# Attention scores as two 64-row matmuls side by side, and one sum instruction for two steps

## The chip, the cores and the metric

The kernel runs on one core of a Trainium2 chip. Its time is the device time of one execution in microseconds (us); shown is the median of several executions. TensorE (PE) multiplies matrices, and its weight loads are listed apart (PEld); VectorE (DVE), ScalarE (ACT) and GpSimd (POOL) do the elementwise work; SyncE (SP) and ScalarE's queue issue DMAs.

## What is computed

Four batches of eight heads of attention over 576 positions with head size 64, with a threshold in the scores, and then two feed-forward layers over all 2304 tokens (512 wide, 2048 inside):

```
scores = (1/sqrt(64)) * q @ k.T                      # per head, 576 x 576
thresh = max(scores, row) - tau
scores = where(scores >= thresh, scores, -1e9)
attn   = exp(scores - max(scores, row)); attn /= sum(attn, row) + 1e-9
x = concat over heads of (attn @ v)                  # 2304 x 512
h = x @ w_in;  x = (relu(h) * relu(h)) @ w_out       # layer 1
h = x @ w2_in; out = max(0.01*h, h) @ w2_out         # layer 2
```

## The kernel before, in words

The two heads of a pair are worked on together. A pair has nine **steps**: four blocks of 128 query rows for each head, and one step that holds the last 64 rows of both heads (the remainder). There are 16 pairs, so 144 steps. `step(i)` issues what leads to the masked row: the scores of 128 query rows against all 576 keys go to a PSUM tile `s` of two banks, 288 keys in each (L585); VectorE takes the row maximum `nb` (L595), ScalarE the exponential `e` (L596), `th` is the threshold (L597, VectorE or GpSimd), VectorE masks and sums (L602), a small instruction `t` adds 1e-9 to the sum and scales it (L605, VectorE or GpSimd), and after every second step a reciprocal `r` of both sums follows (L608). There are two tiles `s`, so a step's scores wait for the mask of the step before last. `rest` then scales the rows, turns them, and `values` multiplies them with v.

The pairs come in three kinds. The first four (batch 0) scale in place, turn the rows with TensorE transposes against an identity matrix into `pt` (L627, L628), copy them to `PT` and multiply with v in single precision, in 64-column matmuls (L688). The first six pairs (list `nat`, steps 0 to 53) have single-precision scores; pairs four and five then use half-precision rows that DMAs turn. The last ten pairs split q and k into a high and a low part; their score matmuls (tiles KH and KL) are not changed.

For the first six pairs `prep` loads K of both heads into one tile KH, head 0 in partitions 0 to 63 and head 1 in partitions 64 to 127, 576 keys wide, and scales it. The tile Q2 holds for each head its 64 rows in the same partitions, with zeros in the other 64 (memsets, L484). A matmul over all 128 partitions thus gives one head's scores; a step issues two, one for each half of the keys. In the remainder step there are four, each with 64 columns of weights.

The order of the work is not written by hand. Every instruction is recorded with a priority (step number plus an offset from the table CFG), a cost, and the engines that may run it; `Plan.order` then simulates the engines and places one instruction after the other, and where several engines may run it the prices in CFG weigh them. Beside the attention run the splitting of layer 1's weights into high and low parts (`w_block`, tiles `wraw`), and from batch 1 on part of layer 1 (`ffn`, L736 and L762). After the attention come the rest of layer 1 (L1166, L1208) and layer 2 (L1055, L1133).

Of the kernel before, what the change touches and what calls it, by code (L numbers as in the profile page):

```python
# [13 lines left out]
ALU = mybir.AluOpType  # L14
# [4 lines left out]
P = 128  # L19
UP = 32768.0  # L20
# [7 lines left out]
           {'V': 2.058, 'A': 0.5, 'G': 0.597},  # L28
           {'V': 1.454, 'A': 0.877, 'G': 1.005},
           {'V': 4.321, 'A': 0.378, 'G': 0.428},  # L30
           {'V': 1.956, 'A': 0.969, 'G': 2.867},
           {'V': 3.46, 'A': 0.884, 'G': 4.561},
           {'V': 3.025, 'A': 1.381, 'G': 2.849}],
    lead1=0.344, xsg0=[0, 1], lbm=8, lb=[[0, 3, 5, 6], [1, 5], [0, 4], [2, 7]], xsm=4, xsg=[1, 2], dq=0.417, xu=False, pqk=-3.957,
    pd1=1.458, pex=1.266, pd2=1.468, ph=3.893, pl=-2.254, hu=True, bg=6.244, lead=4.309, w0=25.544, wstep=1.408, fend=1.015, tol=-0.227,
    hor=-0.102, xlead=5.334, nb=3, eb=4, pb=3, ptb=3, kvb=3, nat=[0, 1, 2, 3, 4, 5], nav=4, two=False, vb=2, tmb=1, gb=2, xb=1,
    w2step=-3.901, nf=[12, 12, 12, 12], wo=2.009, wold=[9, 10, 16], yal=40.578, xl2=26.294, xp=5, sp=2.609, ws=-16.879, ww=20.813, zc=3.74,
    th=0.397, x2l=2.921, sg0=1.043, sgstep=1.158, zb=1.416, zin=1.434, zout=1.386, slack=0.02, slackd=0.985, wrb=3, r1b=1, xrb=1,
# [226 lines left out]
def mmr(n):  # L265
    return (n + 32) / 2400.0
# [11 lines left out]
def tile_kernel(ctx: ExitStack, tc: tile.TileContext, qT, kT, vv, w1, w2, tau, eye, out):  # L278
    nc = tc.nc
    B, H, D, S = qT.shape  # L280
# [4 lines left out]
    S2 = S // 2  # L285
    MAIN = S // P
    REM = S - MAIN * P
    NH = (S + P - 1) // P
    QB = S + REM
# [47 lines left out]
    def dma(o, i, r, w, prio, nbytes, q=nc.sync, **k):  # L337
        return op(("S", 0.06, lambda: q.dma_start(out=o(), in_=i())), r, w, prio, dma=move(nbytes), **k)
# [126 lines left out]
    def prep(n):  # L465
# [6 lines left out]
        o.Q, o.pad = Q, []  # L472
# [3 lines left out]
        if n in CFG["nat"]:  # L476
# [3 lines left out]
            for h in range(2):  # L480

                c0, c1 = (0, S) if len(what) > 5 else (0, 2 * P) if what is head and h == 0 else (REM, REM + 2 * P) if what is head else (2 * P, S) if h == 0 else (0, S)
                z = lambda h=h, c0=c0, c1=c1: qs(h)[(1 - h) * D:(2 - h) * D, c0:c1]
                zero = [("V", 0.55, lambda z=z: nc.vector.memset(z(), 0.0)), ("G", 0.57, lambda z=z: nc.gpsimd.memset(z(), 0.0))]  # L484
                if n:
                    op(zero, [], [Q], at(-1))
                else:
                    zq = Val()
                    o.pad = o.pad + [zq]
                    op(zero[1], [], [zq], at(-1))  # L490
                o.q[h] = c0, c1
            for h in range(2):
                c0, c1 = o.q[h]
                dma(lambda h=h, c0=c0, c1=c1: qs(h)[h * D:(h + 1) * D, c0:c1], lambda h=h, c0=c0, c1=c1: qT[b, h0 + h][:, c0:c1], [], [Q], at(0), D * (c1 - c0) * 4, q=nc.sync if n or h else nc.scalar, urgent=n == 0, issue=0.5 if n or h else 0.06)
            dma(lambda: f32(kh.get()), lambda: kT[b, h0:h0 + 2].rearrange("h d s -> (h d) s"), [], [kh], at(0) if n else -3.1, 2 * D * S * 4, urgent=n == 0)
# [67 lines left out]
    def step(i):  # L563
# [7 lines left out]
        if h is not None:  # L571
            q0 = h * (QB + REM) + t * P
            lhs = [(h, slice(0, P), slice(q0, q0 + P))]
        elif o.KL:
            lhs = [(0, slice(0, P), slice(MAIN * P, MAIN * P + P)), (1, slice(0, P), slice(S, S + P))]
        else:
            lhs = [(0, slice(0, REM), slice(MAIN * P, S)), (1, slice(REM, P), slice(QB, QB + REM))]

        def qk(g):
            if o.KL:  # L580
                ops = [(r, q, kk[hh]) for hh, r, q in lhs for kk in (o.KH, o.KL)]
            else:
                ops = [(r, q, o.KH[hh]) for hh, r, q in lhs]
            for k, (r, q, kk) in enumerate(ops):
                nc.tensor.matmul(ps.get()[r, g, 0:S2], lhsT=o.Q.get()[:, q], rhs=(kk.get() if o.KL else f32(kk.get()))[:, g_(g)],  # L585
                                 start=k == 0 or not o.KL, stop=k == len(ops) - 1 or not o.KL)
        heads = [hh for hh, _, _ in lhs]
        ks = [o.KH[0]] if o.KL is None else [k for hh in heads for k in (o.KH[hh], o.KL[hh])]
        for g in range(2):
            op(("T", 0.486 if o.KL is None and h is not None else 0.58 if o.KL is None else 2 * len(lhs) * mmr(S2), lambda g=g: qk(g)), [o.Q] + o.pad + ks, [ps], i + CFG["pqk"], True)  # L590
# [8 lines left out]
        if not k:  # L599
# [5 lines left out]
        op([(g, c_, lambda eng=eng: eng.tensor_scalar(out=t_.get()[:, k:k + 1], in0=sm.get()[:, k:k + 1], scalar1=1e-9, scalar2=1.0 / UP, op0=ALU.add, op1=ALU.mult), "t")  # L605
            for g, c_, eng in (("V", 0.148, nc.vector), ("G", 0.192, nc.gpsimd))], [sm], [t_], i + CFG["pd2"], True)
        if k:
            op(("V", 0.16, lambda: nc.vector.reciprocal(out=r_.get(), in_=t_.get())), [t_], [r_], i + CFG["pd2"], True)  # L608
# [743 lines left out]
```

## Time and profile before

| | |
|---|---|
| median of 3 executions | 1021.36 us (1020.47 to 1024.64) |
| the profiled execution | 1027.67 us, of which the span from first to last instruction is 1025.9 us |
| mean granted TensorE clock | 0.994 of full speed |
| PE, PEld | 977.7 us (95%), 848.7 us (83%) |
| DVE, ACT, POOL | 841.9 us (82%), 707.7 us (69%), 374.9 us (37%) |
| chain that ended last | PE 66%, DVE 12%, ACT 8%, DMA 5%, issue 5%, POOL 2% |
| score matmuls L585 with KH | 125.6 us in 440 records; with KL 200 more, 56.5 us |

The shares of the span average stages that differ: the attention steps end near 470 us, and the second half is feed-forward work alone. So the profile is read by stretches of time. A single-precision matmul is listed as two passes, each with a weight load; the passes overlap in their recorded times, so that the time from one start to the next is shorter than the duration of one.

### The profile page before, as it was taken

Reading aid. Unit: us, or ns where it says so; the run is one execution under the profiler, and the core shown is the slowest. Engines: PE = TensorE matmul, PEld = TensorE weight load, DVE = VectorE, ACT = ScalarE, POOL = GpSimd, SP = SyncE. Lnnn points to the kernel's source line nnn. Section 1 sums busy time; section 2 is a strip of 40 time slices with the busy share of each in tenths; the row PEclk is TensorE's granted clock in tenths of the full one; section 3 lists DMA queues with packets and bytes.
Section 4 is the critical chain, followed back from the end, with each engine's and each line's share of the span. In section 5 each row is a group of like instructions: output and inputs, shape, how many; then the busy total and the mean of one; then the engine's idle time right before and its main releaser. Section 6 shows DMA issues by size and latency. Waiting matters only on the chain.

```text
span 1025.9 us, 20803 instructions
## 1 busy us (share of the span) xinstructions
PE 977.7 (95%) x7436; PEld 848.7 (83%) x7436; DVE 841.9 (82%) x1944; ACT 707.7 (69%) x1379; POOL 374.9 (37%) x476
## 2 busy tenths in 40 slices
PE   7889899889999989999999999999999999999997
PEld 4545578888889978998988888878888888888897
DVE  6988988889999978873675799899979859858756
ACT  5867878877878778884666897867637636536343
POOL 5776888775778679983310000000000000000000
PEclk9999999999999999999999999999999999999999
DMA  6544599988899789756575554430010020010000
GB/s 190 152 147 111 132 211 197 178 158 170 159 167 181 139 175 181 131 102 131 197 250 185 171 184 144 162 126 22 2 63 21 1 84 1 2 63 1 22 23 22
DMA packets 197688, 122.03 MB, mean 119 GB/s; under 512 B 156752, under 2 KB 175312, under 8 KB 197584
## 3 DMA queue, kind: packets, MB, share of 16 engines
q1 hardware_dynamic: 197216, 120.48, 49.2%
q8 instruction: 59, 0.97, 0.4%
q14 instruction: 45, 0.37, 0.1%
q10 hardware_dynamic: 368, 0.21, 0.1%
HBM read 70.98 MB, written 17.83 MB: 87 GB/s over the span
## 4 chain that ended last, share of the span: by engine, by line
PE 66%; DVE 12%; ACT 8%; DMA 5%; issue 5%; POOL 2%; SPq 1%; DVEq 0%; ACTq 0%; POOLq 0%
PE y L1133 9%; PE h L1166 8%; PE y L1208 8%; PE h L1055 7%; PE y L1055 7%; PE h L1133 7%; PE y L762 6%; PE h L736 5%; PE s L585 5%; DVE e L602 3%; DMA PT<-P 3%; DVE nb L595 2%; ACT e L596 2%; DVE P L649 2%; PE o L683 2%
## 5 line engine op out<-in xcount | busy, mean ns | idle before, releaser
L585 PE MATMUL s<-KH,Q 128*128 128x288 f32 (+1 forms) x440 | 125.6, 379 | 23.9 <-DVE e L602 19.5
L596 ACT ACTIVATE e<-s,nb 128x576 f32<-128x576 f32 x144 | 105.6, 738 | 49.2 <-DVE nb L595 31.9
L602 DVE SCALAR_TENSOR_TENSOR e<-s,th,e 128x576 f32<-128x576 f32 x144 | 116.7, 811 | 22.5 <-ACT e L596 16.4
L595 DVE TENSOR_REDUCE nb<-s 128x1 f32<-128x576 f32 x144 | 107.6, 749 | 18.9 <-PE s L585 18.4
L585 PEld LDWEIGHTS s<-KH,Q 128*128 128x128 f32 (+1 forms) x440 | 74.4, 187 | 45.3 <-issue 22.4
L649 DVE SCALAR_TENSOR_TENSOR P<-e,r,P 128x576 f16<-128x576 f32 x81 | 85.7, 1062 | 11.7 <-ACT P L616 10.1
L896 POOL MEMSET yo<- 128x128 f32 x5 | 1.0, 205 | 222.8 <-DVE b L1063 91.3
L683 PE MATMUL o<-PT,V 128*128 128x320 f16 (+1 forms) x432 | 63.3, 292 | 6.4 <-DVE vbound L537 2.9
L1082 ACT ACTIVATE b<-b 128x1024 f32<-128x1024 f32 (+1 forms) x40 | 38.9, 971 | 34.1 <-DVE b L329 33.9
L1133 PEld LDWEIGHTS <-gh 128*128 128x128 f16 x560 | 54.5, 98 | 6.1
L329 DVE TENSOR_TENSOR b<-b 128x256 f32<-128x256 f32 (+1 forms) x120 | 45.3, 389 | 14.9 <-ACT b L1082 14.4
L318 ACT CAST gh<-b 128x512 f16<-128x512 f32 (+1 forms) x77 | 43.5, 564 | 19.1 <-DVE b L329 18.6
L585 PE MATMUL s<-KL,Q 128*128 128x288 f32 x200 | 56.5, 297 | 0.0
L683 PEld LDWEIGHTS <-V 128*128 128x128 f16 x432 | 40.0, 100 | 19.1 <-issue 7.0
L616 ACT ACTIVATE P<-e,r 128x576 f16<-128x576 f32 x55 | 42.4, 773 | 17.3 <-DMA PT<-P 16.3
L329 DVE TENSOR_TENSOR gl<-b,gh 128x384 f16<-128x384 f32 x80 | 48.8, 614 | 0.2 <-ACT gh L318 0.2
L318 ACT CAST xh<-xr 128x512 fp32r<-128x512 f32 (+3 forms) x66 | 37.8, 582 | 15.4 <-DVE xr L329 13.5
L318 ACT CAST gh<-r 128x512 fp32r<-128x512 f32 (+1 forms) x71 | 42.8, 607 | 4.4 <-DVE r L1174 3.6
L331 POOL TENSOR_TENSOR gl<-r,gh 128x512 fp32r<-128x512 f32 x29 | 40.3, 1389 | 10.0 <-ACT gh L318 5.6
L1063 DVE TENSOR_TENSOR b<-h,b 128x256 f32<-128x256 f32 (+1 forms) x96 | 35.3, 372 | 5.5 <-PE h L1055 3.6
L329 DVE TENSOR_TENSOR xl<-xr,xh 128x512 f16<-128x512 f32 (+3 forms) x58 | 37.7, 651 | 1.6 <-ACT xh L318 1.1
L585 PEld LDWEIGHTS s<-KL,Q 128*128 128x128 f32 x200 | 38.4, 192 | 0.0
(1134 smaller groups left out, 3465.6 us busy)
## 6 DMA issues: line engine op xcount, KB each, us to landing
wraw<-w SPq DMA_DIRECT2D x64, 512.0 KB, 4.1
wraw<-qT SPq DMA_DIRECT2D x20, 288.0 KB, 4.1
wraw<-kT SPq DMA_DIRECT2D x20, 288.0 KB, 4.4
out<-yo SPq DMA_DIRECT2D x18, 256.0 KB, 2.3
VA<-vv SPq DMA_DIRECT2D x32, 128.0 KB, 2.8
x2d<-yo SPq DMA_DIRECT2D x16, 256.0 KB, 2.4
xr<-x2d SPq DMA_DIRECT2D x4, 1024.0 KB, 6.2
y1d<-ys SPq DMA_DIRECT2D x14, 256.0 KB, 2.4
```

The lines of the kernel that those rows point to most:

```text
L318: alts.append(("A", act(n, psum), lambda: nc.scalar.copy(o(), i()), kind))
L329: alts.append(("V", dve(n), lambda: nc.vector.tensor_tensor(out=o(), in0=a(), in1=b(), op=alu), kind + "*"))
L585: nc.tensor.matmul(ps.get()[r, g, 0:S2], lhsT=o.Q.get()[:, q], rhs=(kk.get() if o.KL else f32(kk.get()))[:, g_(g)], start=k == 0 or not o. ...
L595: op(("V", 0.75, lambda: nc.vector.tensor_reduce(out=nb.get(), in_=pv(), axis=AX.XY, op=ALU.max, negate=True)), [ps], [nb], i + CFG["pd1"] ...
L596: op(("A", 0.74, lambda: nc.scalar.activation(e.get(), pv(), AF.Exp, bias=nb.get(), scale=1.0)), [ps, nb], [e], i + CFG["pex"], True)
L602: op(("V", 0.82, lambda: nc.vector.scalar_tensor_tensor(out=e.get(), in0=pv(), scalar=th.get(), in1=e.get(), op0=ALU.is_ge, op1=ALU.mult, ...
L649: op(("V", 0.8, lambda: nc.vector.scalar_tensor_tensor(out=lo(), in0=ev(), scalar=r_.get()[:, k:k + 1], in1=hi(), op0=ALU.mult, op1=ALU.su ...
L683: nc.tensor.matmul(ps.get()[:, 0:w], lhsT=o.V16.get()[:, k if k < NH else k - NH, h].rearrange("p a d -> p (a d)"), rhs=parts16(pt)[:, k, ...
L1055: nc.tensor.matmul(ps.get()[:, 0:w], lhsT=half(wt)[:, ct + kc * P:ct + (kc + 1) * P], rhs=xt(k)[:, kc], start=fresh and q == 0, stop=q == ...
L1133: nc.tensor.matmul(y.get()[:, c * h:(c + 1) * h], lhsT=l, rhs=r, start=first and c == 0 and q == 0, stop=last and c == len(ks) - 1 and q == 2)
L1166: nc.tensor.matmul(ps.get()[:, 0:n], lhsT=a.get()[:, kc * P:(kc + 1) * P], rhs=x.get()[:, kc, 0:n], start=(q == 0 and kc == 0), stop=(q == ...
L1208: nc.tensor.matmul(o(), lhsT=l, rhs=r, start=(first and q == 0), stop=(last and q == 2))
```

## The change

For the first six pairs Q and K are laid out anew. Both halves of the partitions now hold the same two heads: partitions 0 to 63 of KH hold both heads against keys 0 to 287, partitions 64 to 127 both heads against keys 288 to 575; Q2 holds q of both heads twice, once in each half. A step's two matmuls then work on 64 partitions each, one on the lower and one on the upper half of the array's rows, and write to the two banks of `s`. The zeros and their memsets go. K is loaded by two DMAs instead of one, Q by two DMAs of twice the size (for the first pair by four instead of two, two on ScalarE's queue and two on SP's). The sum's small instruction `t` handles both columns of a pair of steps at once, in the second step only. Some thirty constants of CFG are new as well.

```diff
-            for h in range(2):
-                c0, c1 = (0, S) if len(what) > 5 else ...
-                z = lambda h=h, c0=c0, c1=c1: qs(h)[(1 - h) * D:(2 - h) * D, c0:c1]
-                zero = [("V", 0.55, ... memset(z(), 0.0)), ("G", 0.57, ... memset(z(), 0.0))]
...
-            dma(lambda: f32(kh.get()), lambda: kT[b, h0:h0 + 2].rearrange("h d s -> (h d) s"), [], [kh], ...)
+            o.q2 = q2 = lambda: Q.get()[:, 0:2 * S].rearrange("p (h s) -> p h s", h=2)
+            o.k2 = k2 = lambda: f32(kh.get()).rearrange("p (h s) -> p h s", h=2)
+            for g in range(2):
+                rows = slice(g * D, (g + 1) * D)
+                dma(lambda g=g, rows=rows: k2()[rows], lambda g=g: kT[b, h0:h0 + 2, :, g * S2:(g + 1) * S2].rearrange("h d s -> d h s"), [], [kh], ...)
+            if n:
+                for g in range(2):
+                    rows = slice(g * D, (g + 1) * D)
+                    dma(lambda rows=rows: q2()[rows], lambda: qT[b, h0:h0 + 2].rearrange("h d s -> d h s"), [], [Q], ...)
...
+        def tiles():
+            for j in range(2):
+                for g in range(2):
+                    rows = slice(g * D, (g + 1) * D)
+                    if h is None:
+                        a, q, r = j, slice((1 - j) * MAIN * P, (1 - j) * MAIN * P + REM), slice(j * REM, (j + 1) * REM)
+                    elif j == 0:
+                        a, q, r = h, slice(h * REM + t * P, h * REM + (t + 1) * P), slice(0, P)
+                    else:
+                        continue
+                    nc.tensor.matmul(ps.get()[r, g, 0:S2], lhsT=o.q2()[rows, a, q], rhs=o.k2()[rows, a], start=True, stop=True)
...
+            op(("T", 0.69, tiles), [o.Q, o.KH[0]], [ps], i + CFG["pqk"], True)
...
-        op([(g, c_, lambda eng=eng: eng.tensor_scalar(out=t_.get()[:, k:k + 1], in0=sm.get()[:, k:k + 1], ...), "t") ...
         if k:
+            op([(g, c_, lambda eng=eng: eng.tensor_scalar(out=t_.get(), in0=sm.get(), ...), "t") ...
             op(("V", 0.16, lambda: nc.vector.reciprocal(out=r_.get(), in_=t_.get())), [t_], [r_], i + CFG["pd2"], True)
```

Two lines of the constants:

```diff
-    lead1=0.344, xsg0=[0, 1], lbm=8, lb=[[0, 3, 5, 6], [1, 5], [0, 4], [2, 7]], ...
+    lead1=0.138, xsg0=[0], lbm=8, lb=[[0, 3, 5, 6], [1, 5], [4, 6], [2, 7]], ...
```

TensorE's order at the start of the first pair, before (`s` scores, `pt` transposes, `o` value matmuls; line numbers behind the change are 7 higher, those of the scores 5 lower):

```order
21 L585 MATMUL s<-KH,Q_131 128x288 x8
22 L627 MATMUL pt<-eye_sb,e 128x128 x4
23 L628 MATMUL pt<-eye_sb,e 128x128
24 L585 MATMUL s<-KH,Q_131 128x288 x2
25 L627 MATMUL pt<-eye_sb,e 128x128 x4
26 L628 MATMUL pt<-eye_sb,e 128x128
27 L585 MATMUL s<-KH,Q_131 128x288 x2
28 L688 MATMUL o<-PT,VA 64x256 x5
29 L627 MATMUL pt<-eye_sb,e 128x128 x4
30 L628 MATMUL pt<-eye_sb,e 128x128
31 L585 MATMUL s<-KH,Q_131 64x288 x4
32 L585 MATMUL s<-KH,Q_131 128x288
```

The same place now:

```order
21 L580 MATMUL s<-KH,Q_135 128x288 x8
22 L634 MATMUL pt<-eye_sb,e 128x128 x4
23 L635 MATMUL pt<-eye_sb,e 128x128
24 L580 MATMUL s<-KH,Q_135 128x288 x2
25 L634 MATMUL pt<-eye_sb,e 128x128 x4
26 L635 MATMUL pt<-eye_sb,e 128x128
27 L580 MATMUL s<-KH,Q_135 128x288 x2
28 L695 MATMUL o<-PT,VA 64x256 x5
29 L634 MATMUL pt<-eye_sb,e 128x128 x4
30 L635 MATMUL pt<-eye_sb,e 128x128
31 L580 MATMUL s<-KH,Q_135 64x288 x4
32 L580 MATMUL s<-KH,Q_135 128x288 x2
```

The sequence is nearly the same; the two matmuls of a step now stay together, and each takes half the rows.

VectorE's order at its first steps, before:

```order
5 L595 TENSOR_REDUCE nb<-s 128x1 x2
6 L602 SCALAR_TENSOR_TENSOR e,sum<-s,th,e 128x576
7 L372 TENSOR_SCALAR wraw<-wraw 128x512
8 L374 SCALAR_TENSOR_TENSOR wraw<-wraw 128x512
9 L602 SCALAR_TENSOR_TENSOR e,sum<-s,th,e 128x576
10 L595 TENSOR_REDUCE nb<-s 128x1
11 L605 TENSOR_SCALAR t<-sum 128x1
12 L597 TENSOR_SCALAR th<-nb,ca 128x1
13 L608 RECIPROCAL r<-t 128x2
```

The same place now:

```order
5 L602 TENSOR_REDUCE nb<-s 128x1 x2
6 L609 SCALAR_TENSOR_TENSOR e,sum<-s,th,e 128x576 x2
7 L372 TENSOR_SCALAR wraw<-wraw 128x512
8 L602 TENSOR_REDUCE nb<-s 128x1
9 L615 RECIPROCAL r<-t 128x2
10 L602 TENSOR_REDUCE nb<-s 128x1
11 L374 SCALAR_TENSOR_TENSOR wraw<-wraw 128x512
12 L609 SCALAR_TENSOR_TENSOR e,sum<-s,th,e 128x576
13 L372 TENSOR_SCALAR wraw<-wraw 128x512
```

The sum `t` and the threshold `th` of these steps are on GpSimd now, and part of the weight splitting stands behind the next step's row maximum.

## Rows read from the trace of the kernel before

**Rows 1.** Busy by stretch: us; PE, PEld, DVE, ACT, POOL; clock, DMA share, GB/s.

```profile
7.00:104.00 97.00, 85.20 (x461) 50.44 (x459) 86.68 (x195) 73.11 (x124) 69.00 (x109) 0.98 0.52 150
...
517.00:1026.00 509.00, 500.93 (x3997) 439.70 (x3996) 413.42 (x994) 314.01 (x665) 7.45 (x20) 1.00 0.23 76
```

**Rows 2.** The same of line L595 alone (row maxima, one a step).

```profile
7.00:104.00 97.00, 26.60 (x36) 0.98 0.52 150
104.00:167.00 63.00, 13.56 (x19) 1.00 0.83 178
167.00:470.00 303.00, 67.42 (x90) 0.99 0.85 159
```

**Rows 3.** Busy time by stretch, finer, columns as in rows 1.

```profile
43.00:57.00 14.00, 13.50 (x81) 7.83 (x79) 13.05 (x34) 13.40 (x25) 12.52 (x18) 1.00 0.60 170
57.00:71.00 14.00, 9.95 (x52) 6.06 (x51) 13.86 (x26) 9.18 (x17) 9.72 (x15) 1.00 0.29 77
71.00:104.00 33.00, 32.45 (x175) 18.91 (x175) 27.56 (x69) 23.23 (x39) 22.71 (x36) 0.95 0.50 148
```

**Rows 4.** Chain of waits by line: 43 to 57, 71 to 104, 104 to 167, 167 to 469 us.

```profile
by line: PE s L585 37.7%; PE o L688 21.6%; PE pt L627 19.3%; DVE wraw L374 8.5%; issue 5.8%; DVE e L602 5.8%; ACT PT L318 5.0%; PE pt L628 3.9%; DVE nb L595 0.3%
...
by line: PE s L585 38.6%; PE o L688 26.0%; PE pt L627 19.2%; issue 5.3%; DVE e L602 4.7%; PE pt L628 4.0%; ACT e L616 2.3%; DVE xs L703 1.0%; DVE t L605 0.4%; DVE r L608 0.3%; DVE nb L595 0.1%
...
by line: issue 11.9%; DMA wraw<-qT 8.1%; ACT e L596 7.5%; PE h L736 7.2%; DVE e L602 6.8%; DMA PT<-P 6.7%; DVE nb L595 5.3%; PE s L585 4.7%; SPq L338 2.9%; ACT e L616 2.6%; ACT PT L318 2.4%; DVE P L649 2.3%; DVE wraw L374 2.3%; ACT r L743 2
...
by line: PE y L762 10.9%; issue 9.9%; DMA PT<-P 9.0%; PE h L736 8.6%; PE s L585 7.6%; DVE P L649 6.1%; DVE e L602 6.0%; PE o L683 4.8%; DVE nb L595 4.5%; ACT e L596 3.9%; DMA wraw<-kT 2.8%; ACT P L318 1.4%; ACT P L616 1.4%; DMA xr<-x1d 1.2%
```

**Rows 5.** Timeline of TensorE: start, us to the last end, engine, line, instruction, records.

```profile
16.60 1.14 PE L585 MATMUL s<-KH,Q 128*128 128x288 f32 x4
17.66 0.65 PE L688 MATMUL o<-PT,VA 128*64 128x256 f32 x4
...
19.25 0.66 PE L627 MATMUL pt<-eye_sb,e 128*128 128x128 f32 x4
...
19.95 0.95 PE L585 MATMUL s<-KH,Q 128*64 128x288 f32 x6
...
21.66 0.60 PE L627 MATMUL pt<-eye_sb,e 128*128 128x128 f32 x4
```

**Rows 6.** Lines L605 and L597: instructions, ns min/median/max, first and last start.

```profile
L605 DVE TENSOR_SCALAR t<-sum x74: 132/145/156, 12.1 to 471.7; 128x1 f32<-128x1 f32 x74
L605 POOL TENSOR_SCALAR t<-sum x70: 190/192/1032, 9.7 to 460.4; 128x1 f32<-128x1 f32 x70
...
L597 DVE TENSOR_SCALAR th<-nb,ca x80: 193/214/217, 12.2 to 469.8; 128x1 f32<-128x1 f32 x80
```

**Rows 7.** Line L484, the memsets of zeros, columns as in rows 6.

```profile
L484 POOL MEMSET Q<- x12: 567/572/737, 0.7 to 104.3; 64x576 f32 x12
```

**Rows 8.** First loads (issues, KB, us to landing), then timeline of the first microseconds.

```profile
KH<-kT SPq DMA_DIRECT2D x1, 288.0 KB, 3.7
Q<-qT ACTq DMA_DIRECT2D x1, 144.0 KB, 4.0
...
0.74 0.39 SPq L338 DMA_DIRECT2D KH<-kT  x1
...
1.18 0.54 ACTq L338 DMA_DIRECT2D Q<-qT  x1
...
4.67 0.15 DVE L436 TENSOR_SCALAR qsc<-tau_sb 128x1 f32<-128x1 f32 x1 [3.54 <-DMA tau_sb<-tau]
...
4.86 0.52 DVE L450 TENSOR_SCALAR KH<-KH,qsc 128x576 f32<-128x576 f32 x1
...
7.17 0.76 DVE L595 TENSOR_REDUCE nb<-s 128x1 f32<-128x576 f32 x1 [1.79 <-PE s L585]
```

**Rows 9.** Busy time by stretch around a fall of the clock, columns as in rows 1.

```profile
66.00:70.00 4.00, 1.83 (x10) 1.37 (x11) 3.96 (x9) 2.69 (x5) 3.05 (x5) 1.00 0.16 36
71.30:74.60 3.30, 3.30 (x14) 1.97 (x13) 2.20 (x7) 0.17 (x2) 2.42 (x4) 0.50 0.87 303
```

## What I expect, and why

> **What bounds the kernel now.** I read the table by stretch first. In the last stretch [rows 1] TensorE is busy 500.93 of 509.00 us, so the second half is a stream of matmuls that the change doesn't touch: whatever is won must be won before it, and then shifts that stream earlier as a whole. Counted by VectorE's row maxima, one a step, 36 steps begin between 7 and 104 us, the other 18 of the six changed head pairs by 167 us, and the remaining 90 by 470 us [rows 2]. In 7 to 104 us (steps 0 to 35, with no layer-1 matmul to fill gaps) VectorE is busy 86.68 and TensorE 85.20 of 97 us [rows 1], which doesn't say which of them sets the pace. Three finer stretches do [rows 3]: from 57 to 71 us VectorE has 13.86 of 14 us and TensorE waits; from 43 to 57 and from 71 to 104 us TensorE has 13.50 of 14 and 32.45 of 33 us, VectorE 13.05 and 27.56. The chain of waits agrees: there it is score matmuls, transposes and value matmuls one behind the other, the score matmuls alone 37.7% and 38.6% [rows 4]. From 104 to 167 us they are only 4.7% of the chain and from 167 to 469 us, mostly of the other, unchanged head pairs, the chain is spread over layer-1 matmuls, DMA transposes and VectorE.
>
> **The score matmuls.** Before, a step issues two matmuls, each recorded as two passes. Four passes of 0.41 us overlap so that the last ends 1.14 us after the first began [rows 5]: start to start is (1.14 - 0.41) / 3 = 0.245 us, and a step costs 4 x 0.245 = 0.98 us. The remainder steps already show two independent halves of the array side by side, there split by columns: six passes end in 0.95 us [rows 5], which is three pairs (0.41 + 2 x 0.27). No row shows a split by rows in this place. Its bounds are full overlap as in those column pairs, 2 x 0.245 = 0.49 us a step, and none, 0.98 us. I take 0.49, the nearest row being one with the same type, length and engine. A remainder step goes from 8 passes in 4 pairs (0.98 us) to 8 in 2 groups of four (0.49), if both splits work at once.
>
> Against that stands the change of shape. Between the 128-column score passes and the 64-column value passes at 17.66 us the array starts late: the last score pass began at 16.60 + 1.14 - 0.41 = 17.33, its successor was due at 17.575 and came at 17.66, 0.09 us later. Four transposes right behind such a change take 0.66 us, behind matmuls of their own shape 0.60 [rows 5]. I price a change of shape at 0.09 + 0.06 = 0.15 us. In the order of steps 0 to 53 the number of changes goes from 60 to 112, because score matmuls and transposes shared a shape and no longer do: 52 x 0.15 = 7.8 us. So TensorE's score work goes from 54 x 0.98 = 52.9 us to 54 x 0.49 + 7.8 = 34.3 us, 18.6 us or 35% less.
>
> The Trainium skill, "TensorE: Matmul & The Clock Gate", section "Packing small matmuls — row/col tiling", reports 3.07 times for four row groups instead of four. Read as 77% of full overlap, an estimate for two groups here would be 0.64 us a step, 42.4 us in all, 20% instead of 35% saved, and the sum below would be about 4 us instead of 5.9 us; no row of this case shows it.
>
> **What of it lies on the path.** From 43 to 57 us score matmuls are 0.377 x 14 = 5.3 us of the chain, 35% of it 1.8 us, but VectorE leaves only 14 - 13.05 = 0.95 us there. From 71 to 104 us they are 0.386 x 33 = 12.7 us, 35% of it 4.4 us, below the 33 - 27.56 = 5.4 us that VectorE leaves. Sum 5.3 us; since VectorE will not pack without a gap I take 4.5. The rest of 7 to 104 us gives nothing: there VectorE's reductions, masks and weight splitting are the next thing late anyway. From 104 to 167 us: 0.047 x 63 x 0.35 = 1.0 us. Least, nothing; most, all 18.6 us.
>
> **The sum instruction.** The 144 small instructions t become 72. On VectorE they go from 74 to 42, and th from 80 to 66: 32 x 0.145 + 14 x 0.21 = 7.6 us of VectorE [rows 6]; GpSimd loses 40 of 70 t and gains 14 th, and is not late. A reciprocal still waits for the later of its two sums, so no link of the chain goes away, only VectorE time. Of the 7.6 us, 2.6 (9 t, 6 th) fall in steps 0 to 35, of which VectorE bounds 14 of 97 us: 0.4 us. 4.8 us fall behind 167 us, where VectorE has 6.1 + 6.0 + 4.5 = 16.6% of the chain [rows 4]: 0.8 us. Together 1.2 us; between 0 and 7.6.
>
> **Loads and zeros.** Twelve memsets of GpSimd go, 0.57 us each [rows 7]; nobody waited for them: 0 gained. Q is now loaded twice, to both halves of the partitions, 288 KB more a pair. From 7 to 104 us DMA engines are busy half the time (0.52) and the loads are issued a pair ahead, so pairs 1 to 5 hide it; if that cover went, 288 KB at the 150 GB/s of that stretch would be 2 us a pair. At the start it isn't covered. The first score matmul waits for the scaling of K (4.86 to 5.38), which waits for K and, last, for tau (used at 4.67) [rows 8]. Now K comes by two DMAs; with one more issue of 0.4 us the second half lands at about 0.74 + 0.39 + 3.7 = 4.8. The second copy of Q is issued behind the first on ScalarE's queue, 1.18 + 0.54 + 4.0 = 5.7 us, against 5.4 now. I add 0.4 us, between 0 and 2 (the second copy's 288 KB at 150 GB/s).
>
> **The clock.** The granted clock fell to half, 1.2 GHz, for 71.3 to 74.6 us, right after 66 to 70 us, in which TensorE had been busy 1.83 of 4 us [rows 9]. With 18.6 us less to do, such stretches can come more often. One fall of 3.3 us and a little at its edges costs at most half of that, 1.7 us, and nothing where VectorE is late. I add 0.4 us.
>
> **New constants.** They shift instructions between engines and the loads by a place or two; counted in the order, layer-1 matmuls stand at the same steps within about 20 matmuls from step 60 on. I take 0, between 5 us either way.
>
> Sum: 4.5 + 1.0 + 1.2 - 0.4 - 0.4 = 5.9 us less. The profiled execution was 1027.67 us (span 1025.9), so it would be 1021.8; it was 6.3 us above the median of 1021.36, from which I subtract the same: **1015.5 us**.
>
> **Rivals.** *The two halves hardly overlap, or VectorE hides all of it.* Then a step costs 0.98 us or the chain simply moves to VectorE, which has 86.68 of 97 us. Only the sum instruction is left: 1021.4 - 1.2 = about 1020. For it speaks VectorE's share, against it the stretch 71 to 104 us, where VectorE has 5.4 us of slack. *All of TensorE's gain reaches the end*: 1021.4 - 18.6 - 1.2 + 0.8 = 1002.4. For it speaks that TensorE is the busiest engine in every stretch but one and everything it does must be done before the end; against it that in steps 0 to 35, whose 97 us would shrink by 35% of 36 x 0.98 us to 84.7, VectorE still needs 86.68 - 2.6 = 84.1. *The clock takes it back*: TensorE, thinner by 18.6 us in the first 167 us, falls to 1.2 GHz again and again. In 7 to 104 us its busy time would go from 85 to about 73 of 97 us. Each drop costs up to 1.7 us; from four more on it eats the gain, and eight more (13.6 us), all where TensorE is late, give 1021.4 - 6.3 + 13.6 = 1028.7. Against it: only one drop in that stretch now, though it has other gaps.
>
> **How the numbers follow.** My forecast 0.58, with its own range 1010 to 1019.5; hidden 0.15; full gain 0.16; clock 0.11. A change of 0.5%, 5.1 us, is about what a measurement of this kernel can tell from none: faster means below 1016.3. Of the forecast's 0.58, 0.36 lie below that and 0.22 within; the hidden case gives 0.14 within and 0.01 below, the full gain 0.16 below, the clock 0.11 above 1026.5. Faster 0.53, same 0.36, slower 0.11. The range runs from 1006 (a good part of the full gain) to 1025 (short of the clock case).
>
> **What would show it.** Right: score passes in pairs with the same start, a step of 0.5 us plus late starts around it; the 37th row maximum comes some 5 us earlier and the 55th some 6, with little more won by 469 us; VectorE above 90% from 10 to 100 us. Wrong: row halves one behind the other; the 37th row maximum at 104 us as before, with VectorE full; more than three more drops of the clock before 167 us; a first row maximum later than 8.5 us (now 7.17 [rows 8]); or a gain that grows between 167 and 469 us, which would be the constants' work and not the matmuls'.

## The result, and the profile after

The changed kernel takes 1030.55 us (median of 8 runs, 1026.05 to 1031.69), the kernel before beside it 1022.32 (8 runs, 1019.24 to 1026.58). The ratio is 1.007, with a 95% interval of 1.0044 to 1.0096: it is 8 us slower, where 1015.5 us and a range up to 1025 had been forecast. The profiled execution took 1030.38 us (span 1028.6), 0.2 below that median; the profiled one of the kernel before, 1027.67, lies 5.35 above its own, so the two traces alone make the loss look smaller than it is.

First the busy time by stretch of the changed kernel, and under it the same of its row maxima alone (columns as in [rows 1, 2]).

```profile
7.00:104.00 97.00, 80.23 (x501) 42.69 (x499) 89.45 (x201) 77.53 (x129) 68.30 (x105) 0.96 0.65 178
104.00:167.00 63.00, 54.01 (x376) 42.13 (x375) 58.12 (x115) 47.90 (x88) 46.11 (x43) 0.92 0.82 169
517.00:1026.00 509.00, 503.03 (x4014) 441.58 (x4012) 411.50 (x985) 318.80 (x677) 9.24 (x22) 1.00 0.23 76
...
7.00:104.00 97.00, 27.67 (x38) 0.96 0.65 178
104.00:167.00 63.00, 12.05 (x17) 0.92 0.82 169
167.00:470.00 303.00, 65.81 (x89) 0.99 0.83 158
```

By 104 us the kernel is two steps ahead (38 row maxima for 36). Counted in VectorE's timeline, the 37th row maximum starts 6.6 us earlier than before (97.7 for 104.3 us), the 55th only 0.7 us (166.7 for 167.4): in the next 63 us nearly all of the lead is lost. The last stretch is the same stream of matmuls. So the gain comes where it was expected, and is gone again before the stream begins. The start of the last row maximum, the last time in its line's row, says it in one number: 469.0 us before (L595), 471.0 now (L602).

```profile
L595 DVE TENSOR_REDUCE nb<-s x144: 730/751/759, 7.2 to 469.0; 128x1 f32<-128x576 f32 x144
...
L602 DVE TENSOR_REDUCE nb<-s x144: 727/747/759, 7.5 to 471.0; 128x1 f32<-128x576 f32 x144
```

The timeline of TensorE shows the score passes that answer to [rows 5] (start, us to the last end, what, how many passes).

```profile
24.23 0.76 PE L580 MATMUL s<-KH,Q 64*128 64x288 f32 x4
24.92 1.66 PE L695 MATMUL o<-PT,VA 128*64 128x256 f32 x10
26.51 0.66 PE L634 MATMUL pt<-eye_sb,e 128*128 128x128 f32 x4
27.00 0.27 PE L635 MATMUL pt<-eye_sb,e 128*128 128x128 f32 x1
27.20 1.26 PE L580 MATMUL s<-KH,Q 64*128 64x288 f32 x8
```

Four passes end in 0.76 us, not 1.14. Two steps in a row take 1.26, so the second adds 0.50 us: the two halves of the array do run side by side.

What is new stands in the rows of the sum instruction `t`, now line L613 on two columns, which answer to [rows 6]: instructions, ns min/median/max, first and last start.

```profile
L613 DVE TENSOR_SCALAR t<-sum x42: 152/420/3190, 32.6 to 473.6; 128x2 f32<-128x2 f32 x42
L613 POOL TENSOR_SCALAR t<-sum x30: 191/192/900, 10.8 to 462.2; 128x2 f32<-128x2 f32 x30
```

One on VectorE took 132 to 156 ns before, never more. Now half of them take more than 420 ns and one 3.19 us; the 42 take 28.1 us in all, where 74 took 10.8. Two places in the timeline show what they wait for (VectorE and GpSimd only).

```profile
60.81 1.38 POOL L331 TENSOR_TENSOR w4il<-wraw,w4ih 128x512 fp32r<-128x512 f32 x1
60.96 1.26 DVE L613 TENSOR_SCALAR t<-sum 128x2 f32<-128x2 f32 x1
62.25 0.17 DVE L615 RECIPROCAL r<-t 128x2 f32<-128x2 f32 x1
...
179.09 0.86 POOL L708 TENSOR_TENSOR xs<-xs,tmp 64x320 f32<-64x320 f32 x1
179.41 3.19 DVE L613 TENSOR_SCALAR t<-sum 128x2 f32<-128x2 f32 x1
179.92 1.28 POOL L331 TENSOR_TENSOR xl<-xr,xh 128x512 fp32r<-128x512 f32 x1
181.17 1.40 POOL L331 TENSOR_TENSOR V<-VA,V 128x640 f16<-128x640 f32 x1
182.63 0.17 DVE L615 RECIPROCAL r<-t 128x2 f32<-128x2 f32 x1
```

At 60.96 us `t` starts while GpSimd is at work, and ends at 62.22, 0.03 us after GpSimd's instruction (60.81 + 1.38 = 62.19). At 179.41 it sits through three of them one behind the other and ends at 182.60, again 0.03 us after the last (182.57). All 29 that took more than 0.2 us end 0.02 to 0.03 us after an instruction of GpSimd; the seven that met no GpSimd work took 169 or 170 ns, and the other six, beside such work, 152 to 187. No program wait explains it, since the data are VectorE's own. The Trainium skill says why that can be: "SBUF — State Buffer", section "Who interferes with whom", has VectorE's two-port modes and GpSimd share one pair of ports that the first of them holds for its whole instruction; "VectorE: DVE Perf Modes", section "What auto-detection actually checks", lets a one-source instruction take the two-port mode when source and destination lie in SBUF with outermost sizes (other than one) both even or equal. The trace agrees in that `t` waits with two columns, and ends 0.03 us after GpSimd; it is silent on the name of the mode. In one point it differs: at 179.41 us `t` had begun before the second and the third of GpSimd's instructions, and both still went first. In four of the 29 waits GpSimd went first in this way.

The chain of waits shows the loss too. Of 167 to 405 us, `t` alone is 4.6% in the changed kernel, 238 x 0.046 = 10.9 us:

```profile
by line: issue 12.4%; DVE e L609 9.8%; DVE P L656 7.7%; PE h L743 7.1%; DVE nb L602 5.2%; ACT e L603 5.2%; PE s L594 4.9%; DVE t L613 4.6%; PE y L769 4.4%; DMA VA<-vv 4.2%; DMA PT<-P 3.9%; PE o L690 3.3%; DMA wraw<-kT 1.9%; DMA xr<-x1d 1.6%
```

### The profile page after: what moved, and what is told of

It reads as the page before. It is cut to its first block, busy times and chain, and to the rows that moved or that the text cites. A ratio compares the mean times of both kernels' runs of the same rounds, so it can differ in the third digit from the quotient of the medians.

```text
span 1028.6 us, 20717 instructions
## 1 busy us (share of the span) xinstructions
PE 964.2 (94%) x7436; PEld 831.6 (81%) x7436; DVE 852.2 (83%) x1892; ACT 709.8 (69%) x1386; POOL 360.6 (35%) x432
## 4 chain that ended last, share of the span: by engine, by line
PE 60%; DVE 19%; ACT 8%; issue 6%; DMA 4%; POOL 3%; SPq 1%; DVEq 0%; ACTq 0%; POOLq 0%
PE y L1140 9%; PE h L1173 8%; PE h L1062 7%; PE y L1062 7%; PE h L1140 7%; PE y L1215 7%; PE y L769 5%; PE h L743 5%; DVE e L609 5%; DVE nb L602 3%; DVE P L656 3%; ACT e L603 2%; DVE t L613 2%; PE o L690 2%; PE s L594 1%
## 5 line engine op out<-in xcount | busy, mean ns | idle before, releaser
L609 DVE SCALAR_TENSOR_TENSOR e<-s,th,e 128x576 f32<-128x576 f32 x144 | 116.4, 811 | 20.2 <-ACT e L603 12.0
L602 DVE TENSOR_REDUCE nb<-s 128x1 f32<-128x576 f32 x144 | 106.3, 747 | 12.1 <-PE s L594 7.2
L594 PE MATMUL s<-KH,Q 128*128 128x288 f32 x200 | 60.6, 319 | 19.7 <-DVE e L609 17.9
L594 PEld LDWEIGHTS s<-KH,Q 128*128 128x128 f32 x200 | 37.7, 188 | 26.5 <-issue 16.1
L580 PE MATMUL s<-KH,Q 64*128 64x288 f32 (+1 forms) x240 | 41.8, 471 | 13.7 <-DVE e L609 9.7
L604 POOL TENSOR_SCALAR th<-nb,ca 128x1 f32<-128x1 f32 x78 | 37.0, 475 | 35.5 <-DVE nb L602 27.1
```

What stands on the lines that cost most here:

```text
L602: op(("V", 0.75, lambda: nc.vector.tensor_reduce(out=nb.get(), in_=pv(), axis=AX.XY, op=ALU.max, negate=True)), [ps], [nb], i + CFG["pd1"] ...
L609: op(("V", 0.82, lambda: nc.vector.scalar_tensor_tensor(out=e.get(), in0=pv(), scalar=th.get(), in1=e.get(), op0=ALU.is_ge, op1=ALU.mult, ...
```

## The experiments

Theory: `t` on two columns waits for GpSimd, and that made the kernel slower. Rivals: the granted clock took the gain back; the new constants' order cost it; the 64-row scores were worth less than worked out. Times are medians, and each ratio is to the kernel before, run beside it.

**a_narrow: VectorE's t as two one-column instructions, the order otherwise that of the changed kernel.**

```
-            op([(g, c_, lambda eng=eng: eng.tensor_scalar(out=t_.get(), in0=sm.get(), ...
+            def two():
+                for c in range(2):
+                    nc.vector.tensor_scalar(out=t_.get()[:, c:c + 1], in0=sm.get()[:, c:c + 1], ...
```

> The changed kernel, but where t falls to VectorE it is issued as two one-column instructions in the same place; everything else, order and constants, as in the changed kernel. Theory 1 (a two-column t on VectorE waits for GpSimd: 42 of them took 28.1 us, 669 ns each, against 146 ns for a one-column t): t on VectorE falls to 84 x 0.146 = 12.3 us, and 4 to 9 us of the 16 come off the time: 1022 to 1027 us. Theory 2 (the loss is the clock, which stood at half for 10.3 us from 113.7 us on): no change, 1029 to 1031 us, the fall still there. Theory 3 (the new constants order the work worse): no change, 1029 to 1031 us.

Measured: 1018.22 us (7 runs), ratio 0.9959 (0.9938 to 0.998). The row of its `t`:

```profile
L615 DVE TENSOR_SCALAR t<-sum x84: 130/144/156, 33.6 to 462.4; 128x1 f32<-128x1 f32 x84
```

Twice as many instructions take 12.2 us and not 28.1; none waits, though GpSimd was at work during 75 of the 84. The kernel is 12.3 us faster than the changed one by the medians, 11.3 by the two ratios, 3.8 us below the range expected, and faster than the kernel before. Every engine's order is otherwise the same, so these 11 to 12 us are the price of the wide `t`. Step by step, the changed kernel's row maximum comes 3.7 us earlier than a_narrow's at the 37th (a_narrow's clock stood at half for 10.2 us from 74.2 us on, the changed kernel's did not fall there), 1.2 us later at the 55th and 11.3 us later at the last: most of the price falls behind 167 us.

**b_wide: the kernel before with the two-column t alone.**

```
-        op([... tensor_scalar(out=t_.get()[:, k:k + 1], in0=sm.get()[:, k:k + 1], ... [sm], [t_], ...)
         if k:
+            op([... tensor_scalar(out=t_.get(), in0=sm.get(), ... [sm], [t_], ...)
```

> The kernel before with the two-column t alone, old constants, old scores. Theory 1: t on VectorE takes 0.4 to 0.8 us each instead of 0.146, and the time rises to 1025 to 1033 us. Theories 2 and 3: 1020 to 1023 us, as before or a little less.

```profile
L606 DVE TENSOR_SCALAR t<-sum x40: 148/684/1805, 31.0 to 481.8; 128x2 f32<-128x2 f32 x40
```

Measured: 1038.69 us, ratio 1.0159 (1.0142 to 1.0176). The loss is there without 64-row scores and without new constants. Its order is planned anew, so the 16 us, above the range expected, are not `t`'s alone.

**i_stride and s_three: what makes t wait?** In i_stride the two sums stand two columns apart; in s_three VectorE's `t` covers three columns, the third a column of zeros. Both keep the order of the changed kernel and of a_narrow.

```
i_stride  -  out=t_.get(), in0=sm.get()
          +  out=t_.get()[:, 0:4:2], in0=sm.get()[:, 0:4:2]
s_three   +  standing["sum"] = [att.tile([P, 3], F32, ...) for i in range(3)], zeroed once
          -  two one-column instructions
          +  nc.vector.tensor_scalar(out=t_.get(), in0=sm.get(), ...)     # 128x3
```

> The changed kernel with the sums and t in every second column of tiles twice as wide: t is still one two-column instruction, but its columns don't lie side by side. If the waiting for GpSimd hangs on the columns being adjacent: t on VectorE about 0.15 to 0.2 us each and 1016 to 1021 us. If it hangs on there being two columns: 0.67 us each as before and 1028 to 1032 us.

> The changed kernel with VectorE's t as one instruction on three columns (the third is a column of zeros beside the two sums, set once at the start by three memsets, and not read behind); GpSimd's t stays on two columns. Every engine in the order of a_narrow, but for 42 fewer instructions of VectorE and the three memsets. Theory that t waited because it had an even number of columns, which VectorE reads in a faster way through the port that GpSimd holds: with three columns no t takes more than 0.2 us, 42 of them about 6.3 us in all (a_narrow 84 with 12.2, the changed kernel 42 with 28.1), and the time is 1012 to 1018. Rival, that any t on more than one column waits: mean about 0.67 us as in the changed kernel, and 1027 to 1031.

Measured: 1027.02 us, ratio 1.0053 (1.0034 to 1.0072), and 1035.44 us, ratio 1.0146 (1.0129 to 1.0163). The row of `t` in i_stride:

```profile
L613 DVE TENSOR_SCALAR t<-sum x42: 148/435/3192, 33.0 to 472.1; 128x2 f32<-128x2 f32 x42
```

And in s_three:

```profile
L617 DVE TENSOR_SCALAR t<-sum x42: 151/592/2478, 33.3 to 476.2; 128x3 f32<-128x3 f32 x42
```

Neither a gap nor an odd count takes the wait away, so my theory of the even count fell. I had read the Trainium skill's condition too narrowly: three columns against three are equal, which it allows too. What counts for `t` in these runs is more than one column. That s_three is slower still than the changed kernel, and above both ranges, is not explained: its 42 take 28.4 us, hardly more than 28.1.

**o_pool: the wide t on GpSimd alone. m_priced: a_narrow's instructions, with the planner told 0.29 us for the two.** Both are planned anew.

```
o_pool    -  for g, c_, eng in (("V", 0.15, nc.vector), ("G", 0.195, nc.gpsimd))
          +  for g, c_, eng in (("G", 0.195, nc.gpsimd),)
m_priced  -  ("V", 0.15, two, "t")
          +  ("V", 0.29, two, "t")
```

> The changed kernel with the two-column t given to GpSimd alone (72 of about 0.19 us, 13.7 us of GpSimd), planned anew; VectorE has no t at all. Theory that the two-column t waits on VectorE for the port that GpSimd holds: on GpSimd itself it costs no such wait (30 of them had a median of 0.192 us in the changed kernel), VectorE's busy time falls by 25 us or more, and the time is 1014 to 1022. Rival, that the pair form itself is what is slow (two steps wait for one t, so each reciprocal and scaling comes a step late): 1026 to 1031 as the changed kernel. Rival, that GpSimd, which also does slow work of 1 us and more between, now makes the steps wait: above 1024, with the reciprocals' idle time ended by GpSimd.

> The changed kernel with t on VectorE as two one-column instructions, and the planner told their price, 0.29 us for both, in place of 0.15; the order is planned anew with it. Theory that the wide t's wait for the shared port was the loss: t on VectorE stays near 0.146 us per column, and the time is that of a_narrow within the spread of orders, 1014 to 1022. Rival, that a_narrow was quick by the luck of its order and that new constants without a matching order cost several us, as d_const's did: 1024 to 1030.

Measured: 1035.88 us, ratio 1.0123 (1.0091 to 1.0154), and 1047.48 us, ratio 1.0238 (1.0207 to 1.0269). Both missed the range of their theory, and m_priced that of its rival too. o_pool's time fits its last rival, that GpSimd makes the steps wait, but VectorE waited for `t` only 3.6 us in all; why it is slow stays open. m_priced does a_narrow's work without any wide `t` on VectorE and takes 29 us more: a new order and choice of engines, with the lower clock that came with it (0.969 to 0.976), can be worth that much here, so only kernels in the same order can price one instruction. That is why the conclusions rest on a_narrow, i_stride, s_three, v_full, k_waits and the pair g_rows_fixed, q_fixed_waits.

**d_const, c_rows, e_rows_newcfg: one part of the change at a time.** The kernel before with the new constants; the kernel before with 64-row scores and their loads, old constants; the changed kernel with one-column `t` each step. All are planned anew.

```
d_const        -  {'V': 2.058, 'A': 0.5, 'G': 0.597}, ...               # against the kernel before
               +  {'V': 2.377, 'A': 0.5, 'G': 0.597}, ...
c_rows         -  {'V': 2.377, 'A': 0.5, 'G': 0.597}, ...               # against the changed kernel, t as in e_rows_newcfg
               +  {'V': 2.058, 'A': 0.5, 'G': 0.597}, ...
e_rows_newcfg  +  out=t_.get()[:, k:k + 1], in0=sm.get()[:, k:k + 1]     # each step, as before
```

> The kernel before with the new constants alone. Theories 1 and 2: 1019 to 1025 us, no difference that can be measured. Theory 3: 1027 to 1035 us.

> The kernel before with the 64-row scores alone (loads and memsets changed too), old constants, one-column t in every step. Theory 1: the gain of the scores stays to the end, 1013 to 1019 us. Theory 2: the thinner TensorE lets the clock fall for 7 us or more before 167 us and the gain is lost, 1021 to 1027 us. Theory 3: 1013 to 1019 us.

> The changed kernel, 64-row scores and new constants, but with the one-column t in every step as before, planned anew. If only the two-column t was at fault: 1015 to 1021 us, like the variant with two one-column t. If the constants fit only the order they were made for: 1022 to 1030 us.

Measured: 1029.18 (ratio 1.0065, 1.0048 to 1.0083), 1025.63 (1.0035, 1.0019 to 1.005) and 1020.52 us (0.999, 0.9974 to 1.0005). The new constants with the old code are slower than before, and so are the old ones with the new scores; together they are as good as before. c_rows fits the range of the clock theory, and its clock stood at half for 17 us between 102 and 127 us. But the three orders differ, so that none of these times is the price of one part.

**v_full and u_serial: what the overlap of the scores is worth, in a_narrow's order.** v_full takes all 128 rows for each score matmul; u_serial takes the lower 64 rows for both.

```
-                    rows = slice(g * D, (g + 1) * D)
+                    rows = slice(0, P)       # v_full
+                    rows = slice(0, D)       # u_serial
```

> a_narrow with each score matmul on all 128 rows of the array (both halves of the keys against both copies of the queries, so a sum of two products that nobody wants; only the time is of interest), one after the other as in the kernel before; every engine in the order of a_narrow, nothing else changed. It is the kernel before's score matmul in the new order, on an array as full as before. Theory of the prediction: a step's scores go back from about 0.76 to 1.1 us, the row maximum no. 36 comes 5 to 9 us later than a_narrow's, the granted clock is 0.994 or more, and the time is 1021 to 1026, so that the 64-row scores are worth 3 to 8 us net of the clock. Rival, that the clock takes the gain back: the row maxima come no more than 2 us later, since the falls near 9 and 74 us are gone, and the time is 1016 to 1020. Rival, that the longer scores delay other engines by more than their own time in this order: above 1027.

> a_narrow with both score matmuls of a step on the lower 64 rows of the array, so that they follow each other and do not run side by side; every engine in the order of a_narrow, nothing else changed. (The second half of the scores is then computed from the first half of the keys; only the time is of interest.) It measures by itself what the overlap is worth. Theory of the prediction, that the overlap is on the path for 5.5 us up to 167 us: a step's scores go from about 0.76 to 1.1 us or more, the row maximum no. 54 comes 3 to 7 us later than a_narrow's, and the time is 1022 to 1026. Rival, that other engines wait anyway: row maxima within 2 us of a_narrow's, 1017 to 1020. Rival, that the fuller TensorE keeps its clock and gives the loss back: the clock rises from 0.986 to 0.992 or more, and the time is 1016 to 1020 although the scores take longer.

v_full: 1023.11 us (12 runs), ratio 1.0007 (0.9987 to 1.0027), 4.9 us above a_narrow. The row of the row maxima, with the last start behind `to`, in a_narrow:

```profile
L602 DVE TENSOR_REDUCE nb<-s x144: 725/749/759, 7.7 to 459.7; 128x1 f32<-128x576 f32 x144
```

And in v_full:

```profile
L602 DVE TENSOR_REDUCE nb<-s x144: 727/753/760, 9.2 to 468.1; 128x1 f32<-128x576 f32 x144
```

The side-by-side scores are worth 4.9 us net of all they cause in this order; by the two intervals, an estimate, 2 to 8 us. The time fits the expectation, the place does not: a_narrow's row maximum comes 1.8 us earlier than v_full's at the 37th, where 5 to 9 were expected, 4.2 at the 55th and 8.4 at the last (the two profiled executions lie 8.5 us apart). The chain of waits by line, 43 to 57 us, shows where from. In v_full score matmuls lead it:

```profile
by line: PE s L580 44.9%; PE o L697 20.1%; PE pt L636 11.5%; DVE w2il L329 6.0%; DVE e L609 5.9%; DVE nb L602 5.4%; PE pt L637 3.1%; DVE wraw L374 2.5%; issue 1.6%; DVE th L604 0.9%; DVEq L712 0.1%
```

In a_narrow they are not in it at all, and VectorE's masks (L609) and row maxima (L602) are:

```profile
by line: DVE e L609 28.0%; DVE nb L602 25.0%; DVE wraw L374 13.2%; issue 8.7%; DVE xs L712 7.7%; DVE w2il L329 7.4%; DVE wraw L372 4.7%; DVE w3il L329 4.3%; DVE r L617 2.0%; DVE th L604 1.4%; DVEq L609 0.2%; DVEq L712 0.1%; DVEq L374 0.1%
```

u_serial: 1039.49 to 1060.17 us (6 runs), ratio 1.0237 (1.0203 to 1.0271), all of them at least 13 us above what was expected. It measures something else. In the profiled execution, the one of 1060.17, TensorE is the bound from 7 to 57 us, and VectorE is busy less than half the time:

```profile
7.00:57.00 50.00, 46.04 (x125) 25.56 (x124) 22.27 (x50) 21.19 (x36) 16.62 (x31) 1.00 0.48 120
```

The clock column reads 1.00 there only because no record of the clock stands before 75.2 us. Its transposes tell more: four of them take 1.12 us at 72 us and 0.66 from 76 us on, in the timeline of TensorE:

```profile
72.47 1.12 PE L636 MATMUL pt<-eye_sb,e 128*128 128x128 f32 x4
76.02 0.66 PE L636 MATMUL pt<-eye_sb,e 128*128 128x128 f32 x4
```

So that execution ran at 1.2 GHz until 75 us, although TensorE was busy 46 of 50 us, more than half of it with 64-row score matmuls one at a time. What the overlap is worth cannot be taken from it.

**k_waits, q_fixed_waits, h_fill, g_rows_fixed: the clock.** g_rows_fixed is the kernel before with 64-row scores alone, each engine in before's order. q_fixed_waits adds 128x128 matmuls of a constant, whose output nobody reads, where its TensorE waited, and six matmuls of zeros before the first scores. k_waits does the same to a_narrow; h_fill puts two into each step of the first four pairs instead.

```
+                busy({0: 5, 4: 3, 9: 3, 18: 3, 24: 6, 27: 3, 31: 3, 33: 3}.get(flips[0], 0))   # k_waits, before a step's transposes
+                nc.tensor.matmul(fill[:, 0:P], lhsT=ones, rhs=ones, start=True, stop=True)     # busy(n): n times this
```

> The kernel before with the 64-row scores and their loads alone, every engine's instructions in exactly the order of before (the memsets stay in their places but clear 64 columns that nobody reads; one-column t, old constants). If the scores pay by themselves and the 1025.6 us of the 64-row scores in a newly planned order was the order: 1012 to 1019 us. If the lower clock takes the gain back whatever the order (granted share falls from 0.997 to about 0.986, 11 us' worth of full clock): 1019 to 1026 us.

> g_rows_fixed (the kernel before with the 64-row scores alone, every engine in the order of before) with the same kind of fillers where TensorE waited in its trace: 6 before the first scores, 8 before those of step 2, 6 before step 3, and 3 to 5 before four of the transposes of the first 34 steps; same order otherwise. Theory that the clock cost g_rows_fixed its time: the falls at 8.4, 32.3 and 73.2 us (34 us at half clock in all) shorten to 15 us or less, the mean clock goes from 0.983 to 0.991 or more, the 4.2 us lost by step 18 go, and the time falls from 1029.7 to 1021 to 1025. Rival, that the old order and constants waste the shorter scores (waits at other engines): row maxima as in g_rows_fixed, 1028 to 1031 whatever the clock.

> The changed kernel with the two one-column t, and in each step of the first four pairs two matmuls of a tile of ones ahead of the scores, into a PSUM bank that nobody reads; same order otherwise. They keep TensorE busy where it would wait. Theory clock: the falls of the clock at 9 to 20 and 74 to 84 us go, the granted share rises from 0.986 to 0.99 or more, and the time falls from 1018.2 to 1011 to 1016 us, although TensorE does about 0.4 us more a step. Theory that the clock only follows idle time and costs nothing: 1018 to 1028 us, the extra matmuls being on the path.

> The changed kernel with VectorE's t as two one-column instructions (as in a_narrow, same order of everything else on every engine), plus 128x128 matmuls of a constant tile that write to a tile nobody reads, put only where TensorE waited in a_narrow's trace: 7 more before the first scores, 8 before the scores of step 2, and 3 to 6 before eight of the transposes of the first 34 steps. Nothing else is changed. Theory that the lower granted clock costs what is left over a_narrow's 1018.2: the falls near 9, 74 and 115 us get shorter or go, the mean granted clock comes back from 0.986 to 0.992 or more, and the time falls to 1012 to 1015 (4 to 6 us per 0.01 of clock, as the runs of one kernel show it). Rival, that the clock is only a sign and the order sets the time: the clock rises and the time stays at 1017 to 1020. Rival, that the fillers stand in the way: the row maximum no. 36 comes 1 us or more later than a_narrow's, and the time is above 1020.

g_rows_fixed: 1029.67 us, ratio 1.0065 (1.0044 to 1.0087), slower than both of its ranges: in the old order the 64-row scores alone cost some 7 us. q_fixed_waits: 1024.95, 1.0019 (1.0002 to 1.0035), as expected. Busy time from 7 to 57 us in g_rows_fixed, the clock third from the end:

```profile
7.00:57.00 50.00, 40.77 (x214) 21.16 (x211) 42.02 (x95) 37.22 (x62) 32.07 (x54) 0.83 0.66 183
```

And in q_fixed_waits:

```profile
7.00:57.00 50.00, 45.25 (x285) 25.66 (x281) 44.53 (x104) 41.00 (x70) 37.19 (x61) 1.00 0.76 203
```

In one order, more TensorE work and more time won: 4.7 us. The kernel before had 0.98 as a mean over 7 to 104 us [rows 1], g_rows_fixed has 0.83 and 0.93 in the two halves of that time. The clock does take from these scores.

h_fill kept the early clock too, but its 1027.39 us (ratio 1.0057, 1.0039 to 1.0075) show fillers that stand in the way: its 37th row maximum comes 5.0 us later than a_narrow's. k_waits gives 1019.18 us (12 runs), ratio 0.9963 (0.9944 to 0.9981), in the range of the rival that the clock is only a sign. Its clock is at 1.00 up to 104 us where a_narrow has 0.90 and 0.89. First a_narrow:

```profile
7.00:57.00 50.00, 42.58 (x253) 22.77 (x254) 43.76 (x99) 39.98 (x68) 32.71 (x54) 0.90 0.70 188
57.00:104.00 47.00, 39.69 (x231) 21.18 (x231) 40.72 (x97) 34.85 (x57) 32.21 (x47) 0.89 0.51 146
```

Then k_waits:

```profile
7.00:57.00 50.00, 45.49 (x305) 26.75 (x305) 45.39 (x102) 41.82 (x71) 35.02 (x57) 1.00 0.72 190
57.00:104.00 47.00, 42.15 (x280) 24.04 (x278) 44.67 (x112) 37.43 (x63) 36.06 (x51) 1.00 0.59 168
```

Its 55th row maximum comes at 159.3 and not 165.5 us, 6.2 us earlier, but the last one only 0.9 us earlier (458.8), and the end no earlier. So behind 160 us the time won was lost again. From 167 to 405 us the DMA engines are busy 0.89 to 0.91 of the time in both, and DMA transposes and loads stand in a_narrow's chain; that this is what holds the rest back was not tested. Over single runs of one kernel time falls with the clock (a_narrow: 1020.68 us at 0.982, 1014.26 at 0.990), but the filled kernel did not follow that line. How much of the clock's cost reaches the end in the changed kernel stays open.

## Why the prediction was wrong

The step that failed is the sum instruction: "32 x 0.145 + 14 x 0.21 = 7.6 us of VectorE", "Together 1.2 us; between 0 and 7.6". I took the duration of the one-column row [rows 6] for the two-column instruction and took no gain at all for the worst case, as if a wider instruction could only save. It saved no VectorE time: the 42 take 28.1 us where I had counted 6.1, because most of them wait for GpSimd. Against two narrow ones in the same place the wide one costs 12.3 us (a_narrow; 11.3 by the ratios), where 1.2 us of gain had been forecast.

The trace of the kernel before would have told. The same integer instruction on 128x512 stands in it twice, L372, most of it beside GpSimd's work, and L883 behind 517 us, beside none of it. First L372:

```profile
L372 DVE TENSOR_SCALAR wraw<-wraw x32: 409/423/2112, 9.6 to 516.4; 128x512 int32<-128x512 int32 x32
```

Then L883:

```profile
L883 DVE TENSOR_SCALAR wraw<-wraw x32: 414/421/431, 518.7 to 616.8; 128x512 int32<-128x512 int32 x32
```

The least and the median agree, the longest is 2112 against 431 ns. This longest one, at 60.68 us, sits through three instructions of GpSimd and ends 0.28 us after the last of them (VectorE and GpSimd only):

```profile
60.21 0.85 POOL L701 TENSOR_TENSOR xs<-xs,tmp 64x320 f32<-64x320 f32 x1
...
60.68 2.11 DVE L372 TENSOR_SCALAR wraw<-wraw 128x512 int32<-128x512 int32 x1
...
61.05 1.46 POOL L615 TENSOR_SCALAR e<-e,r 128x576 f32<-128x576 f32 x2
```

So the row of a VectorE instruction had a wait for GpSimd in it, and it is of the kind that the change widens.

The other steps, point by point:

- *Two halves side by side, 0.49 us a step*: right, 0.50 between two steps in a row.
- *5.5 us of it on the path, 0.4 lost to the clock*: the sum came out, -5.1 predicted, -4.9 by v_full and a_narrow (2 to 8), and VectorE is next, as forecast (the two chains above). But that is in part luck. Nearly all of the gain was to come by 104 us; the traces of v_full and a_narrow have 1.8 us by the 37th row maximum and 4.2 by the 55th. The clock was priced by one fall of 3.3 us; a_narrow's fell three times for 10.2 us before 167 us, and k_waits, without the first two of these falls, was 6.2 us ahead at the 55th. And in the old order the same scores cost some 7 us (g_rows_fixed).
- *Start and loads*: +0.4 us predicted, first row maximum at 7.5 for 7.2 us, +0.3.
- *Constants*: 0, between 5 us either way. v_full, which has the new constants, the new order and the paired `t` without its wait, is at 1.0007 (0.9987 to 1.0027) of before: nothing that can be told. With the old code and its own new order d_const was 0.65% slower, so this holds for the two together.
- *A win before 104 us shifts the stream as a whole*: right for the stream behind the last row maximum, not for the way to it: k_waits lost 5.3 of its 6.2 us between the 55th row maximum and the last. From the last row maximum to the end of the span are 556.9 us before, 557.6 after, 557.4 in a_narrow and 557.5 in v_full.

Step by step from the kernel before to v_full, a_narrow and the changed kernel: 1022.3 + 0.8 (rest) - 4.9 (scores) + 12.3 (`t`) = 1030.5 us. The last two steps are each one edit in one order; the first is not, and holds whatever the order did. The medians stem from separate series, and each step is uncertain by some 3 us. The rival "the clock takes it back" named a time, 1028.7, that is near, and its cause exists. But a_narrow, whose clock fell for longer (30.7 us in all before 167 us, against 17.1 in the changed kernel), is 12.3 us faster, so the clock was not what made the kernel slower.

## What to carry to other kernels

Before one instruction takes the place of two, look in the trace for the same kind of instruction on more than one column while GpSimd works, and read its longest time, not its median. The fastest version here is a_narrow, 1018.2 us, 0.4% under the kernel before (k_waits is level with it): the 64-row scores kept, VectorE's sum instruction left narrow. Price an edit between kernels in one and the same order; a new plan of order and engines moved this one by up to 29 us.

## What the runs showed of the hardware

- A two-column float32 instruction of VectorE (`t`), 0.17 us where GpSimd was idle, took up to 3.19 us beside GpSimd's work, through three of its instructions, two of which began after it; the one-column form never took more than 0.156 us beside the same work. The reciprocal on two columns beside it never waited: 72 of them took 0.145 to 0.167 us in the changed kernel.
- In u_serial's profiled execution TensorE stayed at 1.2 GHz until 75 us, though busy 46.04 of the 50 us from 7 to 57, more than half of it with single 64-row score matmuls. With the same matmuls in pairs (a_narrow) the clock was at 2.4 GHz from 5.9 us on, but fell for 10.2 us three times (at 9.3, 74.2 and 115.2 us); with 128-row ones (v_full) it first fell at 119.8 us.
